# First stage of an attention and two-layer kernel: v in array halves, separate sums, and bank order

## The chip, the cores and the metric

The kernel runs on one core of a Trainium2 chip. The metric is the device time of one execution in microseconds (us); lower is better. TensorE multiplies, ScalarE (ACT), VectorE (DVE) and GpSimd (POOL) work elementwise, SyncE (SP) issues most DMAs. SBUF is the working memory, PSUM (eight banks of 128 x 512 float32) takes what TensorE writes.

## The reference

Attention with a soft cap over 4 batches, 12 heads, 448 tokens, 64 columns, then two layers on the 1792 x 768 result:

```python
scores = cap * tanh((q @ k.T / sqrt(64)) / cap)
attn = exp(scores - max); attn = attn / (sum(attn) + 1e-09)
x = (attn @ v) laid out as 1792 x 768
h = x @ moe_w_in;  x = (h * cos(h)) @ moe_w_out        # 768 -> 2048 -> 768
h = max(x @ moe2_w_in, 0);  out = (h * h) @ moe2_w_out
```

All is float32. The maximum need not be subtracted while the cap is at most 40; a second path, `general`, does it otherwise and isn't run with these inputs.

## The kernel before, in words

The layers run in two windows of two batches. Large matmuls are done as three float32r matmuls (high times high, high times low, low times high; `mm3`, L530), one pass each. A window is: hidden layer with cosine (`layer(True)`), output layer into `part` (`layer_out(o_part)`), the same again into the next layer's input (`o_x`), then twice `layer(False)` with squared relu and `layer_out`, the last with `o_y`, which adds, transposes (`y_tr`) and stores.

**First stage.** The first twelve head pairs (`NA` = 12, batches 0 and 1) are computed by `a_first` before the layers; the pair's number is n. The other twelve are woven into window 0's layers by `a_steps` and use other forms. The 448 tokens of a head lie in partitions as 64 rows of 4 and 64 of 3; so keys form groups g = 0, 1, 2 of 128 for each of the two heads j, and a group 3 of 64 for each, which share one tile (head 0 in partitions 0 to 63, head 1 above). `a_score` makes scores with k stationary: for groups 0 to 2 each head's 64 contraction rows are one half of the array's rows, for group 3 the full array. ScalarE does tanh, then exp (`a_exp`). `a_av` multiplies with v stationary as plain float32, which is two passes per matmul. A v tile has 128 columns: 64 of v and 64 of ones, so that a head's bank holds the product in partitions 0 to 63 and 64 equal copies of the sum of exponentials above (L404; L407 for group 3, in row halves). `a_out` transposes the sums in VectorE's 32 x 32 blocks to have one per partition, takes the reciprocal, spreads it back and multiplies, one head at a time (L417 to L429). `a_prep(n + 1)` transposes the next pair's q and k on TensorE into the banks that pair n's product is to have next, so it waits for the pair before that to be multiplied out. Weights of the layers are prepared in slots (`w_slot`) on ScalarE and VectorE. All instructions are issued in the order written; each engine keeps that order.

TensorE's order for pair n: scores of groups 0 and 1; transposes for n + 1; av of pair n - 1, group 2; scores of groups 3 and 2; av of n - 1, group 3; av of n, groups 0 and 1. The last pair's rest (`a_last`) stands in the first layer, after its first tile.

**Banks.** `bS` (4), `bM` (2), `bA` (2). Each call of `layer` and `layer_out` takes the banks of its own ring from the ring's first on (`ring[k % len(ring)]`): `layer(False)` has sixteen tiles on `bM` and `bS[3]`, `layer_out` after it twelve on the same three, or on `bM` and `bS` for the last.

In `o_x` GpSimd makes the low half of the next layer's input (L632). In `y_tr` both stores are issued by SyncE.

Of the kernel before, what the change touches and what calls it, by code (L numbers as in the profile page):

```python
# [11 lines left out]
F32 = mybir.dt.float32  # L12
# [16 lines left out]
def tile_softcap_attention_moe_cos_moe_relu2(  # L29
# [199 lines left out]
    def rows_a(t, b, h, n=1):  # L229
        return t[b, h:h + n, 0:TA, :].rearrange("h (r c) d -> r c h d", c=4)  # L230

    def rows_b(t, b, h, n=1):
        return t[b, h:h + n, TA:S, :].rearrange("h (r c) d -> r c h d", c=3)
# [13 lines left out]
        return t if g < 3 else t[:, 0:1]  # L247


    vf = [at_p.tile([P, 7, P], F32, name=f"vf{i}", tag=("q2", "k2")[i]) for i in range(2)]  # L250

    def v_of(n):
        return vf[n % 2]
# [24 lines left out]
    def a_loadv(n):  # L278
        b, p = divmod(n % (B * NP), NP)
        h = 2 * p  # L280
        if n < NA:
            t = v_of(n)
            for j in range(2):
                nc.sync.dma_start(out=t[0:RA, 3 * j:3 * j + 3, 0:D], in_=rows_a(v, b, h + j)[:, 0:3, 0])
                nc.sync.dma_start(out=t[RA:P, 3 * j:3 * j + 3, 0:D], in_=rows_b(v, b, h + j)[:, :, 0])
                nc.sync.dma_start(out=t[RA * j:RA * j + RA, 6, 0:D], in_=rows_a(v, b, h + j)[:, 3, 0])
            return
        vr = at_p.tile([P, 7, D], F32, name="vr", tag="vr")
        v6 = vr[:, 0:6].rearrange("p (h c) d -> p h (c d)", h=2)
        va = v[b, h:h + 2, 0:TA, :].rearrange("h (r c) d -> r h (c d)", c=4)  # L290
        vb = v[b, h:h + 2, TA:S, :].rearrange("h (r c) d -> r h (c d)", c=3)
        nc.sync.dma_start(out=v6[0:RA], in_=va[:, :, 0:3 * D])
        nc.sync.dma_start(out=v6[RA:P], in_=vb)
        for j in range(2):
            nc.sync.dma_start(out=vr[RA * j:RA * j + RA, 6], in_=rows_a(v, b, h + j)[:, 3, 0])
        vraws[n] = vr
# [99 lines left out]
        pts[n, g] = ((vh, ph), (vl, ph), (vh, pl))  # L396

    def a_av(n, g):
        todo = pts.pop((n, g)) if n >= NA else ((v_of(n), t_of(n, g)),)
        for i, (a, x) in enumerate(todo):  # L400
            for j in range(2):
                first, last = g == 0 and i == 0, g == 3 and i == len(todo) - 1
                if g < 3:
                    nc.tensor.matmul(acc(n)[j][:, :S], a[:, 3 * j + g, :], x[:, j], start=first, stop=last)  # L404
                else:
                    r = slice(RA * j, RA * j + RA)
                    nc.tensor.matmul(acc(n)[j][:, :S], a[r, 6, :], x[r, 0], start=False, stop=last)  # L407

    xts = {}

    def a_out(n):
        st = at_p.tile([P, S], F32, name="st", tag="st")
        xts[n] = xx = at_p.tile([P, S], F32, name="xx", tag="xx")
        rc = at_p.tile([P, S // 32], F32, name="rc", tag="rc")
        for j in range(2):
            o = slice(RA * j, RA * j + RA)
            nc.vector.transpose(out=st[o], in_=acc(n)[j][RA:P, :S])  # L417
        sums = st.rearrange("p (a b) -> p a b", b=32)[:, :, 0]
        if tops.pop(n, None) is not None:
            nc.vector.tensor_scalar(out=rc, in0=sums, scalar1=1e-9, scalar2=None, op0=ALU.add)  # L420
            sums = rc
        nc.vector.reciprocal(out=rc, in_=sums)
        nc.vector.transpose(
            out=st.rearrange("p (a b) -> p a b", b=32),
            in_=rc.rearrange("p (a o) -> p a o", o=1).to_broadcast([P, S // 32, 32]),
        )
        for j in range(2):
            o = slice(RA * j, RA * j + RA)
            nc.vector.tensor_tensor(out=xx[o], in0=acc(n)[j][0:RA, :S], in1=st[o], op=ALU.mult)  # L429
# [19 lines left out]
    def a_first(n):  # L449

        slots = iter(W_SLOTS if n else ((),) * 4)
        for g in range(2):
            a_score(n, g)
        if n == 0:
            a_load(2)
            a_loadv(1)
        if n + 1 < NA:
            a_prep(n + 1)  # L460
            if 0 < n and n + 2 < B * NP:
                a_load(n + 2)
        w_slot(next(slots))
        for g in range(2):
            a_exp(n, g)
        w_slot(next(slots))
        if n > 0:
            a_av(n - 1, 2)
        a_score(n, 3)
        a_score(n, 2)  # L470
        if n > 1:
            a_x(n - 2)
        if n > 0:
            a_av(n - 1, 3)
            a_out(n - 1)
        a_exp(n, 3)
        w_slot(next(slots))
        a_exp(n, 2)
        w_slot(next(slots))
        for g in range(2):  # L480
            a_av(n, g)
        if 0 < n and n + 1 < B * NP:
            a_loadv(n + 1)

    def a_last(n):
        a_x(n - 1)
        for g in range(2, 4):
            a_av(n, g)
        a_out(n)
        a_x(n)  # L490

# [83 lines left out]
    def split_g(b, i, u):  # L575
        nc.scalar.copy(out=gh[b][i], in_=u)  # L576
        nc.vector.tensor_tensor(out=gl[b][i], in0=u, in1=gh[b][i].bitcast(F32), op=ALU.subtract)  # L577

    def layer(first, weave=None):
        ring = bM + bA if first else bM + bS[3:]  # L580
        w0 = wpos[0]
        order = [(i, b) for i in range(FB) for b in range(WB)]
        if weave is not None:
            ring = bS[:1] + 4 * ring
            order[1:3] = [(1, 0), (0, 1)]
        for k, (i, b) in enumerate(order):
            if weave is None or i > 1:
                if b == 0:
                    w_next(WB * NCC * 3)
            elif k == 0:  # L590
                w_next(0)
            wh, wl = wsp[w0 + i]
            ps = ring[k % len(ring)][:, :S]
            for c in range(NCC):
                mm3(ps, wh[:, c], wl[:, c], xh[b][c], xl[b][c], c == 0, c == NCC - 1)
            if weave is not None and k == 2:
                w_next(NCC * 3)
            tick()
            (cos_a if first else relu_a)(b, i, ps)
            if k == 0 and weave is not None:  # L600
                weave()

    def layer_out(done, w=None):

        ring = bM + (bS[3:] if w is None else bS)
        w = NWIN if w is None else w
        for d in range(NCC):
            if w + 1 < NWIN:
                for b in range(WB):
                    x_back((w * WB + WB + b) * NP + d)  # L610
            for e in range(FB // OP):
                w_next(WB * OP * 3)
                wh, wl = wsp[wpos[0] - 1]
                for b in range(WB):
                    ps = ring[(WB * d + b) % len(ring)][:, :S]
                    for c in range(OP):
                        f = e * OP + c
                        mm3(ps, wh[:, c], wl[:, c], gh[b][f], gl[b][f], f == 0, f == FB - 1)
                    tick()
                    if e == FB // OP - 1:  # L620
                        done(b, d, ps)
# [4 lines left out]
    def o_x(b, d, ps):  # L626
        t = part[d][:, b]
        u = mo_p.tile([P, S], F32, name="u", tag="u")
        nc.scalar.copy(out=u, in_=ps)
        nc.vector.tensor_tensor(out=t, in0=u, in1=t, op=ALU.add)  # L630
        nc.vector.tensor_copy(out=xh[b][d], in_=t)  # L631
        nc.gpsimd.tensor_tensor(out=xl[b][d], in0=t, in1=xh[b][d].bitcast(F32), op=ALU.subtract)  # L632

    def o_y(w):
        def done(b, d, ps):
# [5 lines left out]
    def y_tr(b, d, y):  # L641
        bk = bA[b % WB]
        for c in range(4):
            m = P if c < 3 else RA
            nc.tensor.transpose(bk[:m, P * c:P * c + P], y[:, P * c:P * c + m], ident)  # L645
        o = at_p.tile([P, 4, P], F32, name="o", tag=("q2", "k2")[b % WB])
        nc.scalar.copy(out=o[0:RA].rearrange("p c f -> p (c f)"), in_=bk[0:RA, :])
        nc.vector.tensor_copy(out=o[RA:P, 0:3].rearrange("p c f -> p (c f)"), in_=bk[RA:P, 0:3 * P])
        t0 = (b % B) * S
        nc.sync.dma_start(  # L650
            out=out[t0:t0 + TA, d * P:(d + 1) * P].rearrange("(r c) f -> r c f", c=4), in_=o[0:RA]
        )
        nc.sync.dma_start(
            out=out[t0 + TA:t0 + S, d * P:(d + 1) * P].rearrange("(r c) f -> r c f", c=3), in_=o[RA:P, 0:3]
        )
# [48 lines left out]
    with tc.manual_schedule():  # L704
# [3 lines left out]
            nc.vector.memset(t[0:RA, 3, 1], 0.0)  # L708
        for t in (qraw, wide_view(pg[0])):
            nc.vector.memset(t[RA:P, 3], 0.0)  # L710
        a_load(0)
        busy(11)
        nc.sync.dma_start(out=capt, in_=cap.partition_broadcast(P))
        make_identity(nc, ident)
        a_load(1)
        a_loadv(0)
        for t in vf:
            nc.gpsimd.memset(t[:, :, D:P], 1.0)
        nc.gpsimd.memset(vh[:, :, D:P].bitcast(F32), 1.0)
        nc.gpsimd.memset(vl[:, :, D:P].bitcast(F32), 0.0)  # L720
        nc.vector.scalar_tensor_tensor(
# [50 lines left out]
```

## Time and profile before

| | us |
|---|---|
| median of 3 runs | 1199.77 (1199.32 to 1201.66) |
| the profiled execution | 1200.93 |
| its span, first to last instruction | 1199.1 |
| TensorE busy | 1180.7 (98%) |
| ScalarE, VectorE, GpSimd busy | 654.1, 664.0, 83.4 |

A busy TensorE is not one at its peak: matmuls are pipelined, and each record reaches to its own end, over the start of the next. So the starts are to be read, not the durations: what one kind of matmul costs is the distance from one start to the next. PEld is TensorE's weight load, which can lie beside a matmul. Idle time of another engine costs nothing unless TensorE waits for it.

### The profile page before, as it was taken

How to read it: one execution, taken by the hardware profiler on the slowest of the kernel's cores; microseconds unless marked ns; L12 is line 12 of the kernel's file. 1: busy time of each engine (PE TensorE's matmuls, PEld its weight loads, DVE VectorE, ACT ScalarE, POOL GpSimd, SP SyncE). 2: the span in 40 equal slices, each digit the busy share in tenths (PEclk: the TensorE clock that was granted, in tenths of full speed). 3: DMA queues.
4: the chain of work that ended last, by engine and by line, in shares of the span. 5: the costliest groups of instructions: out<-in, count | busy, mean ns of one | idle time of the engine just before them, and what ended most of it. 6: DMA issues, size and time to landing. Idle time of an engine off the chain costs nothing.

```text
span 1199.1 us, 15735 instructions
## 1 busy us (share of the span) xinstructions
PE 1180.7 (98%) x5835; PEld 1035.6 (86%) x5835; DVE 664.0 (55%) x1075; ACT 654.1 (55%) x1092; POOL 83.4 (7%) x86
## 2 busy tenths in 40 slices
PE   9999999999999999999999999999999999999996
PEld 5555899999988888999888999999999998999896
DVE  3886796689999888678777754400442111001121
ACT  6987674377866999677885435512541243124301
POOL 1000000000322110001001210000002100000000
PEclk9999999999999999999999999999999999999998
DMA  5544356754556545556645874234223422342152
GB/s 128 139 101 114 129 201 210 253 212 176 183 161 212 189 145 166 161 167 197 208 148 179 267 238 150 88 105 144 101 72 110 154 88 79 117 139 88 53 150 69
DMA packets 163333, 179.65 MB, mean 150 GB/s; under 512 B 64400, under 2 KB 130464, under 8 KB 163248
## 3 DMA queue, kind: packets, MB, share of 16 engines
q1 hardware_dynamic: 162256, 178.26, 46.9%
q8 instruction: 48, 0.79, 0.3%
q10 hardware_dynamic: 928, 0.23, 0.1%
q14 instruction: 37, 0.30, 0.1%
q0 software_dynamic: 64, 0.07, 0.0%
HBM read 119.93 MB, written 58.59 MB: 149 GB/s over the span
## 4 chain that ended last, share of the span: by engine, by line
PE 94%; DVE 4%; ACT 1%; issue 0%; DVEq 0%
PE bM L524 45%; PE bS L524 23%; PE bA L524 9%; PE bA L404 5%; PE bS L355 3%; PE bS L347 2%; PE bM L404 2%; PE bA L407 1%; PE bS L303 1%; PE bA L645 1%; DVE st L417 1%; DVE xx L429 1%; ACT part L360 0%; PE bM L303 0%; PE bS L700 0%
## 5 line engine op out<-in xcount | busy, mean ns | idle before, releaser
L524 PE MATMUL bM<-g,ws 128*128 128x448 f32 x1344 | 289.7, 368 | 4.8 <-ACT u L571 4.8
L524 PEld LDWEIGHTS bM<-g,ws 128*128 128x128 f32 x1344 | 252.1, 188 | 28.3 <-ACT u L571 6.3
L524 PE MATMUL bM<-xh,ws 128*128 128x448 f32 x912 | 268.3, 366 | 0.2 <-DVE xh L631 0.2
L524 PE MATMUL bS<-g,ws 128*128 128x448 f32 x960 | 210.7, 368 | 0.0
L524 PEld LDWEIGHTS bS<-g,ws 128*128 128x128 f32 x960 | 178.7, 188 | 15.2
L524 PEld LDWEIGHTS bM<-xh,ws 128*128 128x128 f32 x912 | 170.9, 188 | 16.2 <-DVE xh L97 0.7
L577 DVE TENSOR_TENSOR g<-u,g 128x448 fp32r<-128x448 f32 x128 | 80.5, 629 | 165.4 <-ACT g L576 165.4
L524 PE MATMUL bM<-xl,ws 128*128 128x448 f32 x456 | 167.4, 367 | 1.4 <-POOL xl L632 1.4
L524 PE MATMUL bA<-xh,ws 128*128 128x448 f32 x372 | 108.7, 366 | 0.0
L561 DVE SCALAR_TENSOR_TENSOR u<-kk,u 128x448 f32<-128x448 f32 x64 | 39.9, 624 | 123.5 <-ACT kk L560 123.0
L169 ACT CAST ws<-wf 128x512 fp32r<-128x512 f32 (+1 forms) x80 | 56.3, 704 | 72.6 <-DVE wf L162 28.3
L170 DVE TENSOR_TENSOR ws<-wf,ws 128x512 fp32r<-128x512 f32 (+1 forms) x80 | 64.1, 801 | 57.3 <-ACT ws L169 55.9
L524 PEld LDWEIGHTS bM<-xl,ws 128*128 128x128 f32 x456 | 85.4, 187 | 9.5 <-POOL xl L632 1.7
L576 ACT CAST g<-u 128x448 fp32r<-128x448 f32 x128 | 71.6, 560 | 8.7 <-DVE u L566 6.9
L524 PE MATMUL bS<-xh,ws 128*128 128x448 f32 x252 | 76.1, 367 | 0.0
L524 PEld LDWEIGHTS bA<-xh,ws 128*128 128x128 f32 x372 | 69.8, 188 | 6.0
L360 ACT ACTIVATE pg<-bS,small 128x448 f32<-128x448 f32 x102 | 59.4, 635 | 20.5 <-PE bS L355 15.7
L524 PE MATMUL bA<-xl,ws 128*128 128x448 f32 x186 | 68.1, 366 | 0.0
L162 DVE CUSTOM_DVE_ANT_0 wf<-wr,wf 128x1024 uint16<-128x1024 uint16 (+1 forms) x80 | 64.7, 808 | 2.0
L159 DVE SCALAR_TENSOR_TENSOR wf<-wr,wf 128x512 uint32<-128x512 uint32 (+1 forms) x80 | 63.7, 796 | 1.7
L154 ACT ACTIVATE wf<-wr 128x512 f32<-128x512 f32 (+1 forms) x80 | 61.4, 768 | 0.1
L624 ACT COPY part<-bM 128x448 f32<-128x448 f32 x32 | 17.1, 534 | 81.4 <-PE bM L524 81.3
(129 smaller groups left out, 1522.4 us busy)
## 6 DMA issues: line engine op xcount, KB each, us to landing
wr<-in_moe_w_in_dram SPq DMA_DIRECT2D x32, 768.0 KB, 4.8
wkeep<-ws SPq DMA_DIRECT2D x32, 768.0 KB, 3.6
wr<-in_moe_w_out_dram SPq DMA_DIRECT2D x48, 512.0 KB, 3.8
wkeep<-ws SPq DMA_DIRECT2D x48, 512.0 KB, 3.5
ws<-wkeep SPq DMA_DIRECT2D x32, 768.0 KB, 4.3
ws<-wkeep SPq DMA_DIRECT2D x48, 512.0 KB, 3.8
out_dram<-o SPq DMA_DIRECT2D x24, 128.0 KB, 2.6
qraw<-in_q_dram SPq DMA_DIRECT2D x22, 128.0 KB, 2.7
```

What stands on the lines that cost most here:

```text
L154: lambda: nc.scalar.activation(out=f, in_=r.bitcast(F32)[:, :n, 1], func=AF.Copy, scale=2.0 ** -112),
L159: lambda: nc.vector.scalar_tensor_tensor(out=u, in0=hi, scalar=0x80000000, in1=u, op0=ALU.bitwise_and, op1=ALU.bitwise_or),
L162: lambda: nc.vector.tensor_tensor(out=u, in0=u, in1=lo, op=ALU.add),
L169: nc.scalar.copy(out=t[:, 0], in_=f)
L170: nc.vector.tensor_tensor(out=t[:, 1], in0=f, in1=t[:, 0].bitcast(F32), op=ALU.subtract)
L355: nc.tensor.matmul(bk[j][:, :S], k[:, j, cols], q2[:, j], start=(i == 0 and (g < 3 or j == 0)), stop=(i == 1 and (g < 3 or j == 1)),)
L360: nc.scalar.activation(out=t_of(n, g)[:, j], in_=bk[j][:, :S], func=AF.Tanh, scale=tsc)
L404: nc.tensor.matmul(acc(n)[j][:, :S], a[:, 3 * j + g, :], x[:, j], start=first, stop=last)
L524: nc.tensor.matmul(o, l, r, start=start, stop=stop)
L561: nc.vector.scalar_tensor_tensor(out=u, in0=kk, scalar=MAGIC, in1=u, op0=ALU.subtract, op1=ALU.subtract)
L576: nc.scalar.copy(out=gh[b][i], in_=u)
L577: nc.vector.tensor_tensor(out=gl[b][i], in0=u, in1=gh[b][i].bitcast(F32), op=ALU.subtract)
```

## The change

For the first twelve pairs the v tile becomes 128 x 4 x 128: for groups 0 to 2 both heads' v side by side (head 0 in columns 0 to 63, head 1 in 64 to 127), and for group 3 a block-diagonal tile with zeros elsewhere. The product of head j goes to partitions 64j to 64j + 63 of one bank, by a matmul of 64 columns. The sums come from separate matmuls with 32 columns of ones (`a_sums`) into quarters of the pair's second bank, two groups per head in each call; `a_out` adds the two quarters of a head. TensorE's order becomes: scores 0 and 1; transposes; av of n - 1, group 3; scores 3 and 2; sums of n - 1 (groups 2 and 3); av of n - 1, group 2; av of n, groups 0 and 1; sums of n (groups 0 and 1). The v loads of a pair are five DMAs instead of six.

The rings of the layers are walked on from call to call by one counter, set to 0 at both ends of `layer(True)` and before the last `layer_out`, whose ring is now `bS[:2] + bM + bS[2:]`. The low half of the last column block in `o_x` is made by VectorE, and the first of the last two stores is issued by ScalarE. The memsets of the v tiles become four small ones on VectorE.

```diff
-    vf = [at_p.tile([P, 7, P], F32, ...) for i in range(2)]
+    vf = [at_p.tile([P, 4, P], F32, ...) for i in range(2)]
+    ones = [t.bitcast(F32) for t in (vh[:, 0, D:D + 32], kz[:, 0, 0:32], kz[:, 1, 0:32])]
...
+            th = t[:, 0:3].rearrange("p c (h d) -> p c h d", h=2)
+            nc.sync.dma_start(out=th[RA:P], in_=rows_b(v, b, h, 2))
+            for j in range(2):
+                o = slice(RA * j, RA * j + RA)
+                nc.sync.dma_start(out=th[0:RA, :, j], in_=rows_a(v, b, h + j)[:, 0:3, 0])
+                nc.sync.dma_start(out=t[o, 3, o], in_=rows_a(v, b, h + j)[:, 3, 0])
...
     def a_av(n, g):
+        if n < NA:
+            av, t = acc(n)[0], t_of(n, g)
+            if g == 3:
+                nc.tensor.matmul(av[:, :S], v_of(n)[:, 3], t[:, 0], start=False, stop=False)
+                return
+            for j in range(2):
+                o = slice(RA * j, RA * j + RA)
+                nc.tensor.matmul(av[o, :S], v_of(n)[:, g, o], t[:, j], start=(g == 0), stop=(g == 2))
+            return
...
+    def a_sums(n, k):
+        for j in range(2):
+            for i, c in enumerate((2 * k, 2 * k + 1)):
+                o = slice(RA * j + 32 * i, RA * j + 32 * i + 32)
+                x = t_of(n, c)[:, j if c < 3 else 0]
+                nc.tensor.matmul(acc(n)[1][o, :S], ones[0 if c < 3 else 1 + j], x, start=(k == 0), stop=(k == 1))
...
     def a_out(n):
+        if n < NA:
+            nc.vector.transpose(out=st, in_=acc(n)[1][:, :S])
+            for i in range(4):
+                o, e = (slice(32 * c, 32 * c + 32) for c in (i, i ^ 1))
+                nc.vector.tensor_tensor(out=rc[o], in0=sums[o], in1=sums[e], op=ALU.add)
+            sums = rc
...
+        if n < NA:
+            nc.vector.tensor_tensor(out=xx, in0=acc(n)[0][:, :S], in1=st, op=ALU.mult)
+            return
...
+    turns = [0]
+    def bank(ring):
+        turns[0] += 1
+        return ring[(turns[0] - 1) % len(ring)][:, :S]
...
     def layer(first, weave=None):
+        if first:
+            turns[0] = 0
...
-            ps = ring[k % len(ring)][:, :S]
+            ps = bank(ring)
...
-        ring = bM + (bS[3:] if w is None else bS)
+        ring = bM + bS[3:] if w is None else bS[:2] + bM + bS[2:]
...
-        nc.gpsimd.tensor_tensor(out=xl[b][d], in0=t, in1=xh[b][d].bitcast(F32), op=ALU.subtract)
+        eng = nc.vector if d == NCC - 1 else nc.gpsimd
+        eng.tensor_tensor(out=xl[b][d], in0=t, in1=xh[b][d].bitcast(F32), op=ALU.subtract)
...
-        nc.sync.dma_start(
+        eng = nc.scalar if b % B == B - 1 and d == NCC - 1 else nc.sync
+        eng.dma_start(
```

## Rows read from the trace of the kernel before

**Rows 1.** The page's first table: busy us, share of the span, instructions.
```profile
PE 1180.7 (98%) x5835; PEld 1035.6 (86%) x5835; DVE 664.0 (55%) x1075; ACT 654.1 (55%) x1092; POOL 83.4 (7%) x86
```

**Rows 2.** Sums by stretch: PE, PEld, DVE, ACT, POOL busy (count), clock, DMA, GB/s.
```profile
61.00:70.40 9.40, 9.26 (x45) 5.32 (x45) 8.19 (x15) 7.71 (x13) 0.00 (x0) 1.00 0.33 74
```

**Rows 3.** Timeline of TensorE where output layers begin: start, us, what [idle <-releaser].
```profile
474.35 0.37 PE L524 MATMUL bM<-xh,ws 128*128 128x448 f32 x1
477.64 4.18 PE L524 MATMUL bM<-g,ws 128*128 128x448 f32 x12 [2.92 <-ACT u L571]
...
646.39 0.36 PE L524 MATMUL bM<-xh,ws 128*128 128x448 f32 x1
647.38 0.88 PE L524 MATMUL bM<-g,ws 128*128 128x448 f32 x3 [0.63 <-ACT u L571]
```

**Rows 4.** Timeline where the first layer without cosine begins.
```profile
388.13 0.47 PE L524 MATMUL bM<-xh,ws 128*128 128x448 f32 x1 [0.24 <-DVE xh L631]
388.22 1.71 POOL L632 TENSOR_TENSOR xl<-part,xh 128x448 fp32r<-128x448 f32 x1 [5.08 <-DVE xh L631]
...
389.99 0.47 PE L524 MATMUL bM<-xl,ws 128*128 128x448 f32 x1 [1.39 <-POOL xl L632]
```

**Rows 5.** Timeline of TensorE over one pair of the first stage.
```profile
70.42 3.27 PE L404 MATMUL bM<-part,vf 128*128 128x448 f32 x8
73.62 1.49 PE L347 MATMUL bS<-g,g 64*128 64x448 f32 x12
75.04 0.66 PE L303 MATMUL bA<-ident,kraw 128*128 128x128 f32 x4
...
75.97 1.67 PE L404 MATMUL bM<-part,vf 128*128 128x448 f32 x4
77.12 1.92 PE L347 MATMUL bS<-g,g 128*128 128x448 f32 x9
78.88 0.91 PE L407 MATMUL bM<-part,vf 64*128 64x448 f32 x4
79.72 0.64 PE L404 MATMUL bA<-part,vf 128*128 128x448 f32 x1
```

**Rows 6.** Timeline of TensorE's weight loads in the same pair.
```profile
71.65 0.19 PEld L404 LDWEIGHTS bM<-part,vf 128*128 128x128 f32 x1 [0.18 <-issue]
...
72.02 0.19 PEld L404 LDWEIGHTS bM<-part,vf 128*128 128x128 f32 x1 [0.19 <-issue]
```

**Rows 7.** The chain that ended last, in the first layer: start, us, what.
```profile
133.25 7.32 PE bA L524 x36
```

**Rows 8.** Timeline of ScalarE, end of pair 2 and begin of pair 3.
```profile
35.04 0.93 ACT L154 ACTIVATE wf<-wr 128x768 f32<-128x768 f32 x1
36.87 0.64 ACT L360 ACTIVATE part<-bS,small 128x448 f32<-128x448 f32 x1 [0.90 <-PE bS L347]
```

**Rows 9.** Timeline of VectorE in the pair of rows 5: `a_out`'s transposes and multiplies.
```profile
70.52 1.34 DVE L417 STREAM_TRANSPOSE st<-bA 64x448 f32<-64x448 f32 x2 [0.61 <-PE bA L407]
...
72.85 1.25 DVE L429 TENSOR_TENSOR xx<-bA,st 64x448 f32<-64x448 f32 x2
```

**Rows 10.** Groups by line: busy us, mean ns | idle before.
```profile
L422 DVE RECIPROCAL rc<-st 128x14 f32<-128x14 f32 x24 | 5.8, 243 | 0.8
```

**Rows 11.** Waits of weight loads: us in total, times, longest us.
```profile
PEld bM L303 <- DVE xx L429: 1.5, 3, 0.5
```

**Rows 12.** Sums by stretch, columns as in rows 2: during and after the longest wait.
```profile
474.60:477.60 3.00, 0.12 (x1) 0.00 (x0) 2.33 (x4) 2.96 (x6) 0.00 (x0) 1.00 0.48 147
477.70:481.60 3.90, 3.90 (x12) 3.47 (x13) 2.15 (x5) 2.52 (x4) 0.00 (x0) 0.60 0.68 224
```

**Rows 13.** Groups by line: the same subtraction on VectorE, first stage.
```profile
L98 DVE TENSOR_TENSOR xl<-xx,xh 128x448 fp32r<-128x448 f32 x12 | 7.5, 626 | 0.4
```

**Rows 14.** Timeline of the last copy and the last store.
```profile
1191.09 0.56 DVE L648 COPY o<-bA 64x384 f32<-64x384 f32 x1 [0.44 <-ACT o L647]
...
1192.03 0.90 SPq L653 DMA_DIRECT2D out_dram<-o  x1
```

More of the change, by code (lines that the diff above doesn't have):

```diff
@@ L247, in t_of @@
         return t if g < 3 else t[:, 0:1]
-    vf = [at_p.tile([P, 7, P], F32, name=f"vf{i}", tag=("q2", "k2")[i]) for i in range(2)]
+    vf = [at_p.tile([P, 4, P], F32, name=f"vf{i}", tag=("q2", "k2")[i]) for i in range(2)]
+    ones = [t.bitcast(F32) for t in (vh[:, 0, D:D + 32], kz[:, 0, 0:32], kz[:, 1, 0:32])]
     def v_of(n):
@@ L282, in a_loadv @@
             t = v_of(n)
+            th = t[:, 0:3].rearrange("p c (h d) -> p c h d", h=2)
+            nc.sync.dma_start(out=th[RA:P], in_=rows_b(v, b, h, 2))
             for j in range(2):
-                nc.sync.dma_start(out=t[0:RA, 3 * j:3 * j + 3, 0:D], in_=rows_a(v, b, h + j)[:, 0:3, 0])
-                nc.sync.dma_start(out=t[RA:P, 3 * j:3 * j + 3, 0:D], in_=rows_b(v, b, h + j)[:, :, 0])
-                nc.sync.dma_start(out=t[RA * j:RA * j + RA, 6, 0:D], in_=rows_a(v, b, h + j)[:, 3, 0])
+                o = slice(RA * j, RA * j + RA)
+                nc.sync.dma_start(out=th[0:RA, :, j], in_=rows_a(v, b, h + j)[:, 0:3, 0])
+                nc.sync.dma_start(out=t[o, 3, o], in_=rows_a(v, b, h + j)[:, 3, 0])
             return
@@ L398, in a_av @@
     def a_av(n, g):
-        todo = pts.pop((n, g)) if n >= NA else ((v_of(n), t_of(n, g)),)
-        for i, (a, x) in enumerate(todo):
-            for j in range(2):
-                first, last = g == 0 and i == 0, g == 3 and i == len(todo) - 1
+        if n < NA:
[3 more added lines that the diff above has]
+                return
+            for j in range(2):
+                o = slice(RA * j, RA * j + RA)
+                nc.tensor.matmul(av[o, :S], v_of(n)[:, g, o], t[:, j], start=(g == 0), stop=(g == 2))
+            return
+        for i, (a, x) in enumerate(pts.pop((n, g))):
+            for j in range(2):
+                first, last = g == 0 and i == 0, g == 3 and i == 2
                 if g < 3:
@@ L414, in a_out @@
         rc = at_p.tile([P, S // 32], F32, name="rc", tag="rc")
-        for j in range(2):
-            o = slice(RA * j, RA * j + RA)
-            nc.vector.transpose(out=st[o], in_=acc(n)[j][RA:P, :S])
         sums = st.rearrange("p (a b) -> p a b", b=32)[:, :, 0]
+        if n < NA:
[4 more added lines that the diff above has]
+            sums = rc
+        else:
+            for j in range(2):
+                o = slice(RA * j, RA * j + RA)
+                nc.vector.transpose(out=st[o], in_=acc(n)[j][RA:P, :S])
         if tops.pop(n, None) is not None:
@@ L467, in a_first @@
         if n > 0:
-            a_av(n - 1, 2)
+            a_av(n - 1, 3)
         a_score(n, 3)
@@ L473, in a_first @@
         if n > 0:
-            a_av(n - 1, 3)
+            a_sums(n - 1, 1)
+            a_av(n - 1, 2)
             a_out(n - 1)
@@ L481, in a_first @@
             a_av(n, g)
+        a_sums(n, 0)
         if 0 < n and n + 1 < B * NP:
@@ L486, in a_last @@
         a_x(n - 1)
-        for g in range(2, 4):
-            a_av(n, g)
+        a_av(n, 3)
+        a_sums(n, 1)
+        a_av(n, 2)
         a_out(n)
@@ L601, in layer @@
                 weave()
+        if first:
+            turns[0] = 0
     def layer_out(done, w=None):
-        ring = bM + (bS[3:] if w is None else bS)
-        w = NWIN if w is None else w
+        ring = bM + bS[3:] if w is None else bS[:2] + bM + bS[2:]
+        if w is None:
+            w = NWIN
+        else:
+            turns[0] = 0
         for d in range(NCC):
@@ L610, in layer_out @@
                     x_back((w * WB + WB + b) * NP + d)
+            sums = []
             for e in range(FB // OP):
@@ L614, in layer_out @@
                 for b in range(WB):
-                    ps = ring[(WB * d + b) % len(ring)][:, :S]
+                    if e == 0:
+                        sums.append(bank(ring))
+                    ps = sums[b]
                     for c in range(OP):
@@ L710, in tile_softcap_attention_moe_cos_moe_relu2 @@
             nc.vector.memset(t[RA:P, 3], 0.0)
+        for t in vf:
+            for j in range(2):
+                nc.vector.memset(t[RA * (1 - j):RA * (1 - j) + RA, 3, RA * j:RA * j + RA], 0.0)
         a_load(0)
@@ L716, in tile_softcap_attention_moe_cos_moe_relu2 @@
         a_loadv(0)
-        for t in vf:
-            nc.gpsimd.memset(t[:, :, D:P], 1.0)
+        for j in range(2):
+            nc.gpsimd.memset(ones[1 + j][RA * j:RA * j + RA], 1.0)
         nc.gpsimd.memset(vh[:, :, D:P].bitcast(F32), 1.0)
```

## The prediction

> **What bounds the kernel now.** I read the page's engine table first, then the sums by stretch, then the timelines of the stretches that the change touches. TensorE is busy for 98% of the span [rows 1], so a saving counts only if it shortens TensorE's own row of work or one of its few waits. The reader is to see three places. In the first stage (the first twelve head pairs, up to about 120 us) one pair takes 9.30 us: in a steady stretch of 9.40 us TensorE is busy for 9.26, ScalarE for 7.71, VectorE for 8.19 [rows 2]. At four changes from the hidden layer to the output layer TensorE waits for ScalarE's reading of a bank [rows 3]. At 388 us it waits for a GpSimd subtraction [rows 4].
>
> **One pair before, from its starts** [rows 5]. From 70.42 to 79.72: eight passes of attention times v, 3.20 us; twelve score passes in row halves, 1.42; eight transposes, 0.93; four passes of av for group 2, then three score passes on the full array and six in halves, 2.91 together; the last four av passes in row halves, 0.84. Sum 9.30. One pass of a float32 matmul comes every 0.376 us (its weight load at 71.65, the next at 72.02; the third digit is from the run of eight) [rows 6], so a matmul, two passes, is 0.752; a layer matmul comes every 7.32/36 = 0.203 us [rows 7]. The eight passes should take 3.01 and take 3.20. What is left, 0.19, is what a change of the tile's shape costs: half before the run (its first weights load in the open), half behind it. The score passes show the same: six pairs at 0.203 are 1.22, and 1.42 go by. A pair before has four such changes. The four passes in row halves (x4 in 0.91 with the last one's tail) take the time of two: two row halves do run side by side, in float32 too.
>
> **The first stage after.** The six matmuls of groups 0 to 2 now stand in column halves (64 columns each), two side by side: three sets of 0.752, where there were six. Group 3 becomes one full matmul, 0.752, where two row halves took the same. The sums, which rode along in the other half of each v tile, now cost matmuls of their own: eight with 32 columns, in two sets of four side by side, 2 x 0.752. So 2.256 + 0.752 + 1.504 = 4.51 stands against 6 x 0.752 + 0.752 = 5.26 before. The order (scores in row halves, full array, row halves, quarters, halves, quarters) has six changes of shape instead of four: 2 x 0.19 more. Net 0.75 - 0.38 = 0.37 us less per pair, 8.93 instead of 9.30, and 12 x 0.37 = 4.4 us.
> No row shows a column tile. The lower bound of a set is 0.752, one matmul's time, as the row halves have it; the upper bound is that nothing overlaps. I take the lower, by the nearest row, the row halves. For a change to or from columns the bounds are 0 and 0.4 (twice the row's price); I take 0.19.
>
> **Does another engine stop the shorter pair?** ScalarE waits 0.90 us before pair 3's first tanh at 36.87, and a weight instruction of 0.93 lies ahead of that [rows 8]: 9.30 - 0.90 - 0.93 = 7.5 us of its own work, below 8.93. Pairs with two weight instructions (7.5 + 1.9 = 9.4 us) overrun by 0.5 once, and TensorE asks for the next pair's first exponentials only behind its scores, transposes and group 3, over 4 us on; what that costs if it lasts is rival D. VectorE loses one transpose and one multiply (1.34 and 1.25 for two each [rows 9]) and gains four additions of 32 x 14: between nothing and the reciprocal's 0.24 each [rows 10]; I take 0.24, since it is as long in the free direction. That is 1.27 off and 1.0 on, so its 8.2 us do not grow. Its chain can also begin 0.94 earlier, since the sums are complete before group 2's set and the change ahead of it, and only its last multiply needs that set; so the three waits of the transposes for it go. They hold the weight loads idle for 0.5 each [rows 11]; some 0.3 of that stands before a change of shape anyway, by my estimate from the 1.42 of the score run, in which the last loads end before the last passes: 3 x 0.2 = 0.6. SyncE issues five v loads instead of six, and the four new VectorE memsets lie ahead of the first transposes, while VectorE waits for the first loads: both nothing; without that cover the memsets would cost at most as much as the four additions, 1.0. First stage: 4.4 + 0.6 = 5.0 us.
>
> **Banks in one turn.** The hidden layer without cosine takes sixteen tiles on three banks, so its last tile has the first bank, and the output layer begun anew with the first bank waits until it is read. Carried on, the next bank was read two tiles before. At 647.38 (and likewise at 1006.84 and 1125.50, the same pattern twice more) the start comes 0.99 us after the last one instead of 0.203, and the first weights load in the open, 0.1: 0.89 x 3 = 2.7 us [rows 3]. At 477.64 it comes 3.29 us later: 3.09 lost. Behind it the granted clock is 0.60 in the mean of 3.9 us (the lower level, 1.2 GHz, for most of it) and twelve matmuls take 4.18 instead of 11 x 0.203 + 0.37 = 2.6: 1.6 more, 4.7 in all [rows 3, 12]. There ScalarE is the one behind (2.96 busy of 3.00 [rows 12]), and TensorE arriving 4.7 us earlier at the woven second attention will meet results that are not yet there. Bounds 0 and 4.7 kept; I take 3.5, nearer to the whole, since ScalarE's own work goes on unchanged and a wait that comes of it later is shared with work that TensorE has in hand. Sum 2.7 + 3.5 = 6.2. The last output layer's ring begins with two banks that the layer does not use, so nothing new is late there.
>
> **Last subtraction on VectorE.** At 388.13 the matmul on xh starts, and the one on xl follows at 389.99 instead of 0.2 later, since GpSimd takes 1.71 us from 388.22. The same shape on VectorE takes 0.626, and its input is there by 388.13: ready near 388.75. So 389.99 - 388.75 = 1.2 us [rows 4, 13]. The other three subtractions that move release nobody who waits today: nothing, against 0.63 us of VectorE each.
>
> **Last store on ScalarE's queue.** The final issue on SyncE starts at 1192.03, though its data is ready at 1191.65, since another issue stands before it [rows 14]: 0.4 us. What follows it on SyncE, up to the span's end, moves along.
>
> **Sum.** 5.0 + 6.2 + 1.2 + 0.4 = 12.8 us. The profiled execution took 1200.93 us (span 1199.1 and 1.8 around it), 1.2 above the median of the runs. 1199.77 - 12.8 = **1187 us**.
>
> **A rule against it.** In the layers a load of 128 columns of weights (0.19 us) goes on under the matmul before it, on the same rows: 36 matmuls in 7.32 us, 0.203 each [rows 6, 7]. The Trainium skill ("TensorE: Matmul & The Clock Gate", Part 3) says that weight loads overlap matmuls in flight only where the row group differs; the trace does not bear that out for the full array, and no run here shows it for column tiles, which all have the same rows. The same part of the Trainium skill gives 2.38 times for three column tiles of 32, which no run here shows either; by that, an estimate, sets of column tiles run at four fifths of full overlap and take 1.0 us more per pair, 12 us in all, about 1199 us.
>
> **Rivals.**
> A, no overlap: column tiles run one after the other, as if nothing had been put side by side. For it: no row shows one. Against: the row halves overlap fully. Price per pair: three more av matmuls and six more of sums, 9 x 0.752 = 6.8; 12 x 6.8 = 81, so 1268 us. It decides from the point where the 14 column matmuls of a pair take over 3.76 + 12.8/12 = 4.8 us, that is, where fewer than 2.2 run at once. Chance 8%.
> B, staggered: the two passes of a matmul keep their order, so a neighbour starts only with the second pass. For it: passes are issued in order. Against: the row halves start in pairs. The six half matmuls take 7 slots of 0.376 instead of 6, each set of quarters 5 instead of 2: 7 x 0.376 = 2.6 per pair, 32 us, 1219 us. Chance 7%.
> C, weights in the open: every column pass waits for its weights, 0.1 as behind a change of shape. Five sets of two passes: 1.04 per pair, 12.5 us, which eats the whole gain: 1199.6. For it: no row shows a column tile's load; against: the layers' rows, where loads go on under matmuls. Chance 7%. (This is what the rule of the Trainium skill above would do.)
> D, the first stage gives nothing: changes to and from columns cost 0.3 each, or ScalarE, already busy for up to 9 us in the weight pairs, sets the pace. Then 7.8 us are left: 1192. Chance 10%.
>
> **How the numbers follow.** The forecast has 68%, with a range of its own from 1180 to 1194: 1180 if changes of shape with narrow tiles are nearly free (4 x 0.15 x 12 = 7 us), 1194 if nothing is kept at 477 us and half of the first stage is lost. D lies inside, C at the upper end, A and B outside. The range 1179 to 1201 leaves out A, B and a little more. Within 0.2% (2.4 us, about what a measurement of this kernel can tell) counts as the same. Faster: 68 + 10 + 1 of C = 79%; same 5%; slower A, B and a part of C, 16%.
>
> **What would show it.** Right: a pair in 8.9 us; column passes that start two and four at a time, 0.376 apart; 0.19 at each change; no wait of the output layer's first matmul on ScalarE, and full clock near 480 us; the span's tail 0.4 shorter. Wrong: column passes with starts one after the other (A, B), 0.48 apart (C), or ScalarE without idle time between pairs (D); a new wait on the split attention weights after 480 us larger than 1 us. If the time is above 1200, the column tiles are the cause.

## The result: 1188.6 us, and the profile after

The changed kernel takes 1188.63 us (median of four runs, 1188.11 to 1188.85) against 1200.62 (1199.32 to 1201.66) for the kernel before on the same chip: ratio 0.990, 95% interval 0.9883 to 0.9917, 12.0 us less. Forecast were 1187 us and 12.8 us less, counted from the 1199.77 of the kernel before's first three runs. The profiled run took 1188.85 us, its span is 1187.1 us, 12.1 less than before. The first table of the page of after answers [rows 1]: busy us, share of the span, instructions.

```profile
PE 1174.2 (99%) x6003; PEld 1022.6 (86%) x6003; DVE 656.5 (55%) x1107; ACT 653.5 (55%) x1092; POOL 76.9 (6%) x82
```

Where the time went is read from the starts of the same layer matmuls in both traces: how much earlier each one comes in the changed kernel, and by how much that lead grows (won) or shrinks (minus) in each stretch.

| stretch (time before) | forecast, us won | measured, us won |
|---|---|---|
| first stage, to the last pair's end (126) | 5.0 | 5.7 |
| first layer and its output (126 to 387) | 0 | -0.9 |
| first layer without cosine begins (387 to 401) | 1.2 | -1.25 |
| its output layer begins (474 to 485) | 3.5 | 4.8 |
| the three later output layers (647, 1007, 1125) | 2.7 | 2.7 |
| tail | 0.4 | 1.0 |
| sum (0.1 more in between) | 12.8 | 12.1 |

**One pair after**, the timeline of TensorE that answers [rows 5]: start, us, what.

```profile
61.18 1.48 PE L352 MATMUL bS<-g,g 64*128 64x448 f32 x12
62.59 0.66 PE L308 MATMUL bM<-ident,kraw 128*128 128x128 f32 x4
63.08 0.60 PE L308 MATMUL bM<-ident,qraw 128*128 128x128 f32 x4
63.52 0.92 PE L408 MATMUL bA<-pg,vf 128*128 128x448 f32 x2
63.93 1.93 PE L352 MATMUL bS<-g,g 128*128 128x448 f32 x9
65.78 0.56 PE L429 MATMUL bA<-pg,vh 128*32 128x448 f32 x1
65.79 0.56 PE L429 MATMUL bA<-pg,kz 128*32 128x448 f32 x1
65.80 0.56 PE L429 MATMUL bA<-pg,vh 128*32 128x448 f32 x1
65.80 0.56 PE L429 MATMUL bA<-pg,kz 128*32 128x448 f32 x1
66.18 0.54 PE L429 MATMUL bA<-pg,vh 128*32 128x448 f32 x1
...
66.67 0.97 PE L412 MATMUL bA<-pg,vf 128*64 128x448 f32 x4
67.47 1.67 PE L412 MATMUL bM<-part,vf 128*64 128x448 f32 x8
69.08 0.96 PE L429 MATMUL bM<-part,vh 128*32 128x448 f32 x8
69.97 1.49 PE L352 MATMUL bS<-g,g 64*128 64x448 f32 x12
```

From 61.18 to 69.97 are 8.78 us (from unrounded starts), where before it was 9.30. The four quarters of a sum start within 0.02 us of each other, and the second pass of all four comes 0.40 us on, since the first stands right behind a change of shape; elsewhere passes come 0.376 us apart. The sums take 66.67 - 65.78 = 0.89, the halves 69.08 - 66.67 = 2.41, the other sums 0.89 again: 0.752, 2.256 and 0.752 and one change of shape each, 0.14 to 0.15.

**Where the first layer without cosine begins**, TensorE's timeline that answers [rows 4]; in brackets the idle time ahead and what ended it.

```profile
383.28 0.47 PE L558 MATMUL bM<-xh,ws 128*128 128x448 f32 x1 [0.19 <-DVE xh L682]
383.94 0.47 PE L558 MATMUL bM<-xl,ws 128*128 128x448 f32 x1 [0.19 <-DVE xl L685]
...
384.86 0.36 PE L360 MATMUL bS<-q,k 128*128 128x448 f32 x1
387.00 0.74 PE L360 MATMUL bS<-q,k 128*128 128x448 f32 x1 [1.78 <-ACT pg L365]
```

The wait for the subtraction is down from 1.39 to 0.19, and a new one of 1.78 stands 3 us behind it: a score matmul of the woven second attention wants a bank that ScalarE's tanh (L365) has not read. The next rows say why, first VectorE's, then ScalarE's.

```profile
383.26 0.62 DVE L685 TENSOR_TENSOR xl<-part,xh 128x448 fp32r<-128x448 f32 x1
383.80 0.95 DVE L162 CUSTOM_DVE_ANT_0 wf<-wr,wf 128x1536 uint16<-128x1536 uint16 x1
```

```profile
384.79 0.83 ACT L169 CAST ws<-wf 128x768 fp32r<-128x768 f32 x1 [4.31 <-DVE wf L162]
385.53 0.90 ACT L154 ACTIVATE wf<-wr 128x768 f32<-128x768 f32 x1
386.34 1.12 ACT L365 ACTIVATE pg<-bS,small 128x448 f32<-128x448 f32 x2
```

The moved subtraction (L685) stands ahead of a weight instruction (L162) on VectorE; ScalarE is idle for 4.31 us until that is done, and only behind two weight instructions of its own comes the tanh that TensorE waits for. TensorE now arrives 1.25 us earlier, and the chain that it meets ends 0.6 later: 1.8. From 386.20 to 389.60 the granted clock is 0.54 in the mean, so at the lower level, 1.2 GHz, for most of that stretch (columns as in [rows 2]):

```profile
386.20:389.60 3.40, 2.60 (x7) 2.34 (x8) 3.37 (x6) 3.34 (x7) 0.00 (x0) 0.54 0.99 352
```

**Where the output layer begins** (answers [rows 3, 12]): no wait, twelve matmuls in 2.61 us instead of 4.18, full clock.

```profile
470.80 0.36 PE L558 MATMUL bM<-xh,ws 128*128 128x448 f32 x1
471.00 2.61 PE L558 MATMUL bM<-g,ws 128*128 128x448 f32 x12
```

```profile
470.00:474.00 4.00, 4.00 (x21) 3.69 (x20) 3.30 (x5) 3.94 (x7) 0.00 (x0) 1.00 0.37 113
```

**Tail** (answers [rows 14]): from the last copy's start to the span's end 7.1 us, 8.1 before. SyncE's last two issues (1.50 us together) no longer wait behind the one that ScalarE took over.

```profile
1179.60 1.50 SPq L708 DMA_DIRECT2D out_dram<-o  x2
1179.99 0.59 ACTq L705 DMA_DIRECT2D out_dram<-o  x1
1179.99 0.56 DVE L701 COPY o<-bA 64x384 f32<-64x384 f32 x1 [0.44 <-ACT o L700]
```

### The profile page after: what moved, and what is told of

Its sections match the earlier page's. It is cut to its first block, busy times and chain, and to the rows that moved or that the text cites. A ratio compares the mean times of both kernels' runs of the same rounds, so it can differ in the third digit from the quotient of the medians.

```text
span 1187.1 us, 16072 instructions
## 1 busy us (share of the span) xinstructions
PE 1174.2 (99%) x6003; PEld 1022.6 (86%) x6003; DVE 656.5 (55%) x1107; ACT 653.5 (55%) x1092; POOL 76.9 (6%) x82
## 4 chain that ended last, share of the span: by engine, by line
PE 98%; DVE 1%; ACT 1%; issue 0%
PE bM L558 46%; PE bS L558 23%; PE bA L558 10%; PE bA L418 4%; PE bS L360 3%; PE bS L352 3%; PE bM L412 1%; PE bA L412 1%; PE bM L429 1%; PE bA L429 1%; PE bS L308 1%; PE bA L698 1%; PE bA L421 1%; PE bA L308 1%; PE bM L308 0%; PE bS L755 0%
## 5 line engine op out<-in xcount | busy, mean ns | idle before, releaser
L170 DVE TENSOR_TENSOR ws<-wf,ws 128x512 fp32r<-128x512 f32 (+1 forms) x80 | 64.1, 801 | 57.6 <-ACT ws L169 57.0
L365 ACT ACTIVATE pg<-bS,small 128x448 f32<-128x448 f32 x102 | 59.5, 638 | 19.9 <-PE bS L360 16.2
L162 DVE CUSTOM_DVE_ANT_0 wf<-wr,wf 128x1024 uint16<-128x1024 uint16 (+1 forms) x80 | 64.6, 808 | 1.9
```

The costliest lines, as they stand in the source:

```text
L162: lambda: nc.vector.tensor_tensor(out=u, in0=u, in1=lo, op=ALU.add),
L170: nc.vector.tensor_tensor(out=t[:, 1], in0=f, in1=t[:, 0].bitcast(F32), op=ALU.subtract)
L365: nc.scalar.activation(out=t_of(n, g)[:, j], in_=bk[j][:, :S], func=AF.Tanh, scale=tsc)
```

## Experiments

All times are medians, with the range of the runs; the kernel before ran on the same chip each time (1200.67 us for e_nobank, e_pool, e_late and e_merge, 1200.17 for e_first, e_order, e_last and e_best_late, 1199.81 for e_tail and e_cast). Diffs are against the kernel after unless said otherwise. How much earlier a kernel is than before is read from the same layer matmuls as above. The first scores start at 8.77 us in the profiled run of before, at 8.83 in that of after, and between 7.4 and 8.9 in the others, though no experiment's edit touches what runs before them; so stretches are compared, not ends.

**e_first: the first stage alone** (banks, subtraction and store as before).

```diff
-        ring = bM + bS[3:] if w is None else bS[:2] + bM + bS[2:]
+        ring = bM + (bS[3:] if w is None else bS)
...
-        eng.tensor_tensor(out=xl[b][d], in0=t, in1=xh[b][d].bitcast(F32), op=ALU.subtract)
+        nc.gpsimd.tensor_tensor(out=xl[b][d], in0=t, in1=xh[b][d].bitcast(F32), op=ALU.subtract)
...
```

> The kernel before with the first stage of the change alone (rings, GpSimd subtraction and last store as before). The first stage is worth 5.7 us in the changed kernel's starts, of which 1.0 is lost again in the first cosine layer, where 36 matmuls take 7.36 instead of 7.32: 1200.7 - 4.7 = 1196.0 us. With the waits of the kernel before at 388 and at the four output layers unchanged. Rival (the first stage's gain is partly the rings' or the subtraction's): above 1197.5.

1195.93 us (1195.41 to 1197.85), ratio 0.9966 (0.9954 to 0.9978): 4.2 us less. By the trace, and counted from the first scores (0.9 early in this run), the gain is 5.4 at the last pair's end and 4.4 at 306 us, and stays at 4.4 to 4.6 from there on. So the first stage brings a little more than the 5.0 that were forecast, and 0.9 to 1.0 of it is lost again in the first layer.

**e_nobank: each output layer begins its ring anew.**

```diff
-            ps = bank(ring)
+            ps = ring[k % len(ring)][:, :S]
...
-        ring = bM + bS[3:] if w is None else bS[:2] + bM + bS[2:]
+        ring = bM + (bS[3:] if w is None else bS)
...
```

> The changed kernel with the rings begun anew in each layer, as before the change; first stage, subtraction and store as changed. If the bank collision is the whole cause of the four waits and of the lower clock near 480 us: 3 x 0.9 + 4.7 = 7.4 more, 1196.0, with the four waits on relu back. Rival (part of the gain came from the shorter first stage, which lets ScalarE catch up): the wait near 470 is shorter than 2 us and the clock stays up, 1192 to 1194.

1195.26 us (1194.46 to 1197.13), ratio 0.9953 (0.994 to 0.9967), 6.6 more than the kernel after. TensorE's waits in this run (us in total, times, longest):

```profile
PE bM L558 <- ACT u L605: 4.8, 4, 2.9
PE bS L360 <- ACT pg L365: 1.8, 1, 1.8
```

The four waits are back, the clock falls at 474 us, and between 474 and 1143 us the kernel wins nothing on the one before (4.7 us earlier at both ends), where the kernel after wins 7.6. The banks are the whole cause of that part, and none of it is given back.

**e_pool: the last subtraction back on GpSimd.**

```diff
-        eng = nc.vector if d == NCC - 1 else nc.gpsimd
-        eng.tensor_tensor(out=xl[b][d], in0=t, in1=xh[b][d].bitcast(F32), op=ALU.subtract)
+        nc.gpsimd.tensor_tensor(out=xl[b][d], in0=t, in1=xh[b][d].bitcast(F32), op=ALU.subtract)
```

> The changed kernel with the last column block's low half back on GpSimd; all else as changed. Theory N (order on VectorE): the moved subtraction stands ahead of a weight instruction (L162) for which ScalarE's weight copy waits, and behind that copy stands the tanh whose bank the woven scores need; so the move's net is a loss. Expected 1187.4 us (1.2 less than the changed kernel's 1188.6), TensorE waits about 1.4 us for GpSimd again near 385, no wait of 1.8 us on the scores, no fall of the clock there. Rival W (TensorE is simply 5 us further ahead of a ScalarE that is behind): the wait on the scores stays at 0.5 us or more beside the GpSimd wait, 1188.6 to 1190.

1188.31 us (1187.71 to 1188.48), ratio 0.9893 (0.9878 to 0.9908): no measurable difference from the kernel after, and not the 1187.4 of the first theory. The waits do move as that theory says (TensorE's timeline):

```profile
385.11 0.47 PE L558 MATMUL bM<-xl,ws 128*128 128x448 f32 x1 [1.39 <-POOL xl L684]
...
386.12 0.95 PE L360 MATMUL bS<-q,k 128*128 128x448 f32 x2
```

But the clock fell behind this 1.39 us too (0.79 in the mean from 384 to 392), which it did not behind the same wait of the kernel before. From 387 to 401 us this kernel loses 0.65 on the one before, the kernel after 1.25; with a fall in both, the wait on VectorE's side is 0.6 dearer in these two profiled runs. So the move to VectorE is a small loss there, not a gain; the time alone could not have told it. The loss is small also because VectorE pays less than the 0.62 us of each subtraction: beside GpSimd's (1.71 us from 383.35) VectorE's addition of the next batch takes 1.55 us, like the 1.56 in the kernel before, and 0.62 in the kernel after (VectorE's timeline, first of the kernel before, then of the kernel after). From the start of its first addition to that of L170 go 3.72 us in e_pool and 4.11 in the kernel after, though the latter has two subtractions more in between.

```profile
388.86 1.56 DVE L630 TENSOR_TENSOR part<-u,part 128x448 f32<-128x448 f32 x1
```

```profile
384.67 0.62 DVE L681 TENSOR_TENSOR part<-u,part 128x448 f32<-128x448 f32 x1
```

**e_late: the same subtraction on VectorE, but behind the weight instruction** (for the first batch, through the list of postponed work).

```diff
+        if eng is nc.vector and b == 0:
+            later(0, lambda: nc.vector.tensor_tensor(
+                out=xl[0][d], in0=part[d][:, 0], in1=xh[0][d].bitcast(F32), op=ALU.subtract
+            ))
+            return
```

> The changed kernel, but the subtraction of batch 0's last column block, still on VectorE, is issued one matmul group later, behind the weight instruction L162. N: the tanh comes 0.6 us earlier, the low half 0.9 later; the wait on the scores falls from 1.78 to below 0.7, the clock stays up, 1186.8 to 1187.6 us. W: the wait on the scores does not depend on VectorE's order, stays above 1.2 us and the time is 1188.6 or more.

1186.83 us (1186.11 to 1187.10), ratio 0.988 (0.9865 to 0.9895), 1.8 less than the kernel after. The wait for the subtraction is 0.93 (0.19 in the kernel after, 1.39 before), the one for the scores 0.37 instead of 1.78; the clock is 1.00 from 384 to 392, and the stretch from 387 to 401 now wins 0.3 on the kernel before:

```profile
384.40 0.47 PE L558 MATMUL bM<-xl,ws 128*128 128x448 f32 x1 [0.93 <-DVE xl L686]
...
386.06 0.47 PE L360 MATMUL bS<-q,k 128*128 128x448 f32 x1 [0.37 <-ACT pg L365]
```

That bears out the chain above: the subtraction's place on VectorE sets when the scores may go on.

**e_merge: both sets of sums in one run**, one turn later, so that a pair has five changes of shape instead of six.

```diff
         if n > 0:
+            a_sums(n - 1, 0)
             a_sums(n - 1, 1)
...
-        a_sums(n, 0)
...
```

> The changed kernel with all sums of a pair in one run (both sets in the next pair's turn, directly ahead of group 2's product): five changes of tile shape per pair instead of six, the same matmuls. If a change to or from columns costs the 0.14 us that the changed kernel's starts show: 11 to 12 x 0.14 = 1.6 us less, 1187.0. If it costs the 0.19 of the row changes: 1186.4. Rival: the sums are complete 0.9 us later against the next transposes, VectorE's chain (3.1 us) becomes late and the transposes wait 0.2 to 0.5 per pair: 1189 to 1193.

1188.15 us (1186.06 to 1188.26), ratio 0.9893 (0.9878 to 0.9908). Most pairs take 8.65 us instead of 8.78, one change of shape less, as expected; the second takes 9.24, and two take 8.79 and 8.83. The set that is moved out of the first pair comes back in the last. Of 12 x 0.13 = 1.6 some 0.8 is left at the last pair's end, counted from the first scores. The median missed the expected 1187.0. The run at 1186.06 is the profiled one, and there the wait of 1.8 us stands, but the clock is 1.00 from 384 to 392; the other three, 2.1 us longer, have a lower mean clock (0.996 against 0.998), which fits a fall there, though they left no trace. The rest of the 2.1 may be the start: the profiled run's first scores come at 7.76, a microsecond earlier than in the kernel after.

**e_order: groups 0 and 1 head by head** instead of both heads of a group in turn.

```diff
...
-        for g in range(2):
-            a_av(n, g)
+        for j in range(2):
+            for g in range(2):
+                a_av(n, g, (j,))
```

> The changed kernel with the four matmuls of groups 0 and 1 issued head by head (both groups of head 0, then both of head 1) instead of group by group; the same matmuls. It asks whether column halves run side by side by themselves or only when neighbours in the order stand in different halves. If a matmul cannot start before its predecessor has: head 0's second matmul waits for its first, and three sets' time goes by instead of two, 0.75 per pair, 9 us, 1197.6; if single passes keep the order, 7 slots instead of 4, 1.13 per pair, 13.5 us, 1202. If TensorE looks past a waiting matmul: no change, 1188.6.

1190.31 us (1188.93 to 1190.63), ratio 0.9912 (0.9897 to 0.9927). In the steady pairs the halves still run side by side, the second head's 0.06 us late, and a pair takes 8.85:

```profile
67.69 0.97 PE L412 MATMUL bA<-pg,vf 128*64 128x448 f32 x4
68.49 1.72 PE L412 MATMUL bM<-part,vf 128*64 128x448 f32 x8
70.14 0.96 PE L429 MATMUL bM<-part,vh 128*32 128x448 f32 x8
```

So a matmul whose half of the array is busy does not hold up a later one for the other half; the theories with sets one after the other (1197.6, 1202) fall. The first pair differs. There the weights of group 1 wait for ScalarE (timeline of the loads, then of the matmuls):

```profile
14.22 0.19 PEld L412 LDWEIGHTS bM<-part,vf 128*64 128x64 f32 x2 [0.64 <-ACT part L390]
15.14 0.20 PEld L412 LDWEIGHTS bM<-part,vf 128*64 128x64 f32 x4 [0.74 <-ACT part L390]
```

```profile
14.22 2.65 PE L412 MATMUL bM<-part,vf 128*64 128x448 f32 x8 [0.26 <-ACT part L390]
```

The eight passes take 2.65 us, 1.90 in the kernel after: at 14.22 only one head's two passes go, and the other head's, whose data is as ready, are not started until the wait ahead of them ends at 15.14. A wait for another engine does hold up all that stands behind it. 0.75 there and ten times 0.06 are 1.4 of the 1.7 us by which this kernel is longer than the kernel after; the stretch from 387 to 401 us, where its clock falls later, loses another 0.3 (1.55 instead of 1.25).

**e_tail: both last stores on SyncE.**

```diff
-        eng = nc.scalar if b % B == B - 1 and d == NCC - 1 else nc.sync
-        eng.dma_start(
+        nc.sync.dma_start(
```

> The changed kernel with both last stores on SyncE again, as before the change. If the second issue on the way is all: SyncE's last issue starts 0.4 later and everything behind it moves along, 1189.0 us. If SyncE's longer last issue (0.90 instead of 0.53) and its flag load behind it count too, as the changed kernel's end shows (last copy to the end of the span 1.0 shorter): 1189.6 us. Rival (the end is set by the stores' landing or another engine's way out): 1188.6.

1189.78 us (1189.21 to 1190.67), ratio 0.9917 (0.9904 to 0.9931), 1.15 more than the kernel after; counted from the kernel before on the same chip it wins 10.0, where the kernel after wins 12.0. In the profiled run SyncE's last issue takes 1.50 us:

```profile
1179.96 1.50 SPq L707 DMA_DIRECT2D out_dram<-o  x1
```

From the last copy's start to the span's end are 8.89 us, 1.8 more than in the kernel after and 0.8 more than in the kernel before; in exchange the clock does not fall near 387, which is worth 0.9. With both stores on SyncE that issue took 0.90 (before), 0.58 (e_first) and 1.50 (e_tail), and the tail 8.06, 7.89 and 8.89. With one on ScalarE it took 0.53 and the tail 7.06 to 7.33, in all nine profiled runs. So the larger of the two readings is nearer, but how much the store is worth differs from run to run: 0.6 to 1.8 by these traces.

**e_last: e_late, and group 3's product last in the last pair**, so that a full-array matmul, not one in halves, precedes the first layer.

```diff
...
-        a_av(n, 3)
         a_sums(n, 1)
-        a_av(n, 2)
+        a_av(n, 2, 3)
+        a_av(n, 3, 3)
...
```

> The kernel with the later subtraction (1186.8), and in the last pair's rest group 3's product (full array) as the last before the layer instead of the first: as many changes of shape, but the layer's matmuls follow a full-array matmul instead of column halves. If the slower first layer (36 matmuls in 7.36 instead of 7.32 us, 1.0 us in all) hangs on what stands ahead of it: 7.32 again and 1185.9. If not: 1186.8.

1186.93 us (1186.53 to 1187.20), ratio 0.9889 (0.9874 to 0.9904), the same as e_late. The first layer still loses 0.9: that a matmul in halves stands just ahead of it is not the cause.

**e_best_late and e_cast: the best version.** The first is e_merge and e_late together; the second adds one edit, the cast ahead of the subtraction on ScalarE, which is idle there.

```diff
+        if b == 0 and d == NCC - 1:
+            nc.scalar.copy(out=xh[b][d], in_=t)
+        else:
+            nc.vector.tensor_copy(out=xh[b][d], in_=t)
```

> Both improvements together: all sums of a pair in one run, and the last subtraction of batch 0 behind the weight instruction. If they add: 1186.8 - 1.6 = 1185.2 us, a pair in 8.65 us, no fall of the clock near 385. Rival: TensorE, 1.6 us further ahead, meets the scores' wait again in full: 1186.5 or more.

> The kernel with the sums in one run and the later subtraction (1186.3), and batch 0's last cast to xh on ScalarE, which idles there for 3.6 us, instead of on VectorE. VectorE reaches the weight instruction and the subtraction 0.39 earlier each. If VectorE's order is what sets both waits near 384 (0.93 on the low half, 0.37 on the scores): together 0.3 to 0.5 less, 1185.9 us. Rival (the cast on ScalarE comes later than VectorE's and holds up the matmul on xh and the subtraction): 1186.3 or more.

e_best_late takes 1186.31 us (1185.30 to 1186.58), ratio 0.988 (0.9865 to 0.9895): 1.1 above what was expected, since merging the sums brings 0.9 on e_late by the traces, not the 1.6 of twelve pairs; the two times are 0.5 apart, and the gains on the kernel before, each on its chip, are the same (13.8 and 13.9). e_cast takes 1185.39 us (1185.03 to 1186.05), ratio 0.9878 (0.9863 to 0.9894). All three waits at 382 to 385 us are short in it:

```profile
PE bS L360 <- ACT pg L365: 0.4, 1, 0.4
PE bM L559 <- ACT xh L684: 0.4, 1, 0.4
...
PE bM L559 <- DVE xl L690: 0.3, 1, 0.3
```

It beats both kernels, the one after by 3.2 us; on the kernel before of its own chip it wins 14.4, where the kernel after wins 12.0.

## Why the prediction was right, step by step

**The column tiles were right, and a little better than priced.** The sets take the lower bound, one matmul's 0.752, with two and with four tiles; rivals A and B (matmuls or passes one after the other) and C (weights in the open) are refuted by the pair's rows above, and the time of e_first says the same. The pair takes 8.78, not 8.93, because the term "changes of shape" was too dear: a change to or from columns costs 0.14 to 0.15, not the 0.19 of the row halves. What was forecast for twelve pairs holds for eleven at most: the last pair takes 8.44 us to the layer's first matmul where it took 8.04 before, and one early pair takes 9.12. There the run of halves takes 2.01 us instead of 1.67, in a stretch with a DMA share of 0.92; first the timeline of the matmuls, then that of the loads in the same pair of e_first, which names the v load as late.

```profile
32.00 2.01 PE L412 MATMUL bM<-part,vf 128*64 128x448 f32 x8
```

```profile
31.72 0.20 PEld L412 LDWEIGHTS bM<-part,vf 128*64 128x64 f32 x3 [0.18 <-DMA vf<-in_v_dram]
```

A shorter pair asks for its v sooner; the prediction had not asked whether that comes in time. ScalarE, rival D's limit, sets no pace: between 15 and 110 us it waits eight times for TensorE's scores, 8.2 us in all. The sum, 5.7 instead of 5.0, is the cheaper change of shape less these two. The transposes' waits for the multiply are gone, as forecast. The small additions take 0.174 each, within the bounds:

```profile
L442 DVE TENSOR_TENSOR rc<-st 32x14 f32<-32x14 f32 x44 | 7.7, 174 | 0.8
```

The rule weighed in the prediction does not hold here. Column tiles all have the same rows, and their loads go on under the passes: the eight passes from 67.47 follow each other in pairs every 0.376 us, and the loads for the next two go on beside the two that run (timeline of the loads):

```profile
67.47 0.14 PEld L412 LDWEIGHTS bM<-part,vf 128*64 128x64 f32 x2 [0.23 <-issue]
67.85 0.14 PEld L412 LDWEIGHTS bM<-part,vf 128*64 128x64 f32 x2 [0.23 <-ACT part L365]
```

By the Trainium skill ("TensorE: Matmul & The Clock Gate", Part 3) such loads would not overlap, and three tiles would give 2.38 times; this trace has four at the price of one.

**The banks were right in place and low in size.** I kept 3.5 of the 4.7 at 477 us because ScalarE, the one behind there, would meet TensorE again at the woven attention; all 4.8 were kept, and no wait follows. That the attention's other matmuls cover what ScalarE is late with would explain it, but no run shows it by itself. The three later ones came at 0.9 each, as worked out.

**The subtraction is the step that failed, and its sign with it.** The prediction took 1.2 us from the wait that goes, and of the subtractions that move it asked only who waits for them. It did not ask what stands behind the first on VectorE. There stands L162, for which ScalarE waits, for whose tanh TensorE waits: a wait of 1.78 in place of 1.39. The stretch lost 1.25 us, of which 0.3 is the longer wait (so much does it lose in e_nobank and e_tail, where the clock stays at 1.00) and the rest the fall of the clock. e_late turns the sign by the order of two instructions alone.

**The store was worth 1.0, not 0.4, in these two runs.** I counted the start that moves, and that is right: the last issue starts 0.59 us behind the last copy's start instead of 0.94. I did not count the issue itself, which takes 0.53 us instead of the 0.90 of [rows 14], nor the 0.3 by which the rest up to the span's end is shorter. With both stores on SyncE the issue took anything from 0.58 to 1.50 (e_first, e_tail), so this part is no fixed gain.

**Unforeseen: the first layer lost 0.9.** In the kernel before, 36 matmuls take 7.32 us up to about 306 us [rows 7], and 7.36 later. In the changed kernel they take 7.36 from the start (the chain that ended last):

```profile
134.92 7.36 PE bM L558 x36
...
630.97 7.36 PE bM L558 x36
```

All changed versions do so, at a granted clock of 1.00. As e_first is among them, it comes with the first stage; e_last rules out the shape of the matmul just ahead; the cause stays open.

So 12.8 against 12.0 hides errors of both signs: first stage, banks and store 2.6 better than forecast, subtraction and first layer 3.4 worse. That the two nearly cancel is luck; the mechanism of the column tiles and of the banks is not.

## What to carry to other kernels

Small matmuls that share all rows (here float32 with 448 columns moved) can be put side by side in column halves or quarters at the price of one, if like shapes stand together; each change of shape cost 0.14 to 0.19 us. When an instruction moves to another engine, read what is queued behind it there, follow that to the bottleneck engine, and place it behind whatever leads there. When a ring of buffers is walked on from call to call instead of anew, the waits that go can be kept in full: here 0.9 three times, and 4.8 at the place where ScalarE, which reads the banks, was busy for all but 0.04 of 3.00 us.

## What the runs showed of the hardware that was not expected

- TensorE starts a matmul for a free half of the array past one that must wait for its own half (e_order, 0.06 us late), but not past one that waits for another engine (0.75 us lost). The Trainium skill ("TensorE: Matmul & The Clock Gate", Part 3) says that matmuls start and end strictly in order; the second case agrees, the first, four passes of each head in 1.72 us together, does not.
- The same wait does not always lower the clock. Behind 1.39 us for the subtraction it fell in e_pool, and not in the kernel before or e_first. Behind 1.8 us for the scores it fell in the kernel after and, later, in e_order, and not in e_nobank, e_tail or the profiled run of e_merge. By 401 us the fall has cost the kernel after 0.9 against e_tail, where the same wait brings none. What decides is open.
- VectorE's additions in `o_x` take 0.62 us alone and 1.55 to 1.58 where GpSimd's subtraction has just begun beside them (before, after, e_pool); its transposes out of PSUM take 0.65 with GpSimd at work beside them or not.
- The layers' spacing has two values at full clock, 7.32 and 7.36 us for 36 matmuls, and a kernel can change from the one to the other on its way.
